# An attention with two MLPs behind it: loads wait for the landing four places ahead, and two first products move into the attention

## The chip, the core and the metric

The kernel runs on one core of a Trainium2 chip. The metric is the time of one execution in device microseconds; lower is better. The core has TensorE (PE in the profile, its weight loads PEld), VectorE (DVE), ScalarE (ACT), GpSimd (POOL) and SyncE (SP), which here only issues transfers. Every engine works through its own instructions in order, and waits on semaphores for the others.

## The reference, cut to what matters

Inputs are q, k and v of shape 2 x 8 heads x 768 x 64 in float32, a decay per head, and the weights of two MLPs of 512 x 2048 and 2048 x 512. The attention runs in blocks of 64 positions with a state that decays from block to block:

```python
for b in range(nb):
    intra = np.einsum('bhic,bhjc->bhij', qb, kb) * Dmask[None]
    intra = np.einsum('bhij,bhjd->bhid', intra, vb)
    inter = np.einsum('bhid,bhde->bhie', qb * lam_pow[None], kv_state)
    out[:, :, sl] = intra + inter
    kv_state = lam_block * kv_state + np.einsum('bhsd,bhse->bhde', kb * rev_pow, vb)
...
h = x @ w_in;  g = h * np.clip(h + 3.0, 0.0, 6.0) / 6.0;  x = g @ w_out     # first MLP
h = x @ w_in;  g = np.maximum(0.01 * h, h);               x = g @ w_out     # second MLP
```

## The kernel before

**Attention.** There are 12 chunks c of 64 positions, each with both batches and all heads. For a chunk TensorE makes three pieces of 16 matmuls each in float32: the scores s(c) into a `pair` bank (`scores`), the state t(c) into an `a` bank (`state`), and the output o(c) into an `h` bank (`attn_out`). A float32 matmul is two matmul records and two weight-load records, so a piece is 64 records. ScalarE copies q into the other halves of the pair bank before s(c) (`queries`, two copies, L314), copies t(c) beside v for the next chunk (`state_copy`, two copies, L336), copies half of an odd chunk's v (`part_v`, L289), and rounds o(c) to the high part xh of x (`att_x`, L353). VectorE masks the scores into r (`mask`, L322) and makes the low part xl. GpSimd multiplies k by the decay (`k_decay`).

**MLPs.** Tokens stand in three tiles of 512 (four chunks each), the 2048 hidden units in 16 slices f. Weights come as 64-bit floats; ScalarE reads both halves of a slice (c at L416, t at L420), VectorE composes a float32 of them in four operations, ScalarE rounds it to wh and VectorE makes the rest, wl. A product then takes three matmuls for one: wh with xh, wh with xl, wl with xh. `gemm1(s)` is the first product of one slice on one token tile, 12 matmuls of 128 x 512; then come a gate (u, Gh, Gl) and the second products into `acc` banks.

**What sets the order.** `Order` is a planner: each operation has an engine, a cost, a due time, predecessors and buffers, and the operations are written out in the order in which the planner starts them. Every engine then keeps that order, and semaphores do the rest. `due1` and `due2` are the due times of first and second products; chunk c is due at `DUE_C[c]`.

**Loads.** Loads of q and k (three of 256 KB for a chunk: q, k for the decay, k for the scores), of v (two of 256 KB for a pair of chunks) and of the first slices (two halves of 256 KB each; later slices one of 512 KB) go through SP in the order of `LOAD_ORDER`. They are numbered here from 0: 0 to 2 are q and k of chunk 0, 3 and 4 v of chunks 0 and 1, and so on. Buffers hold four chunks of q and k, three pairs of v and three raw slices. The landings are told by eight semaphores in turn, so that load n also waits for the landing of load n - 8. TensorE's records are counted (`records`), and a border is put 8 records past record 193 and every 256 records after it. From load 15 on, six loads each wait for the first matmul behind a border; the planner is told of it by `AT_BORDER`.

Of the kernel before, what the change touches and what calls it, by code (L numbers as in the profile page):

```python
# [9 lines left out]
F32 = mybir.dt.float32  # L10
# [26 lines left out]
DUE_C = [5.0 + 3.5 * c for c in range(NSC)]  # L37
T_FIRST, T_STEP, T_COLLECT, HOP = 40.0, 5.45, 2.0, 0.3
LATENCY = {"dma": 2.5, "pe": 0.15, "act": 0.15, "dve": 0.15, "pool": 0.15}
N_WARM, T_WARM = 9, 4.4  # L40
N_DENSE = {("s", 0): 5}
NQ = 4

FIRST_BORDER, BLOCK, PAST_BORDER = 193, 256, 8
FIRST_LOADS, LOADS_PER_BLOCK = 15, 6
AT_BORDER = (('o', 0), ('o', 1), ('s', 4), ('t', 4), ('o', 5), ('s', 8), ('t', 8), ('o', 9))
LOAD_ORDER = (('qk', 0), ('v', 0), ('qk', 1), ('qk', 2), ('v', 2), ('qk', 3), ('qk', 4), ('v', 4), ('qk', 5), ('qk', 6), ('v', 6), ('qk', 7), (0, 0, 0), ('qk', 8), ('v', 8), ('qk', 9), ('qk', 10), ('v', 10), (0, 0, 1), ('qk', 11))


class Order:  # L50
# [7 lines left out]
    def add(self, engines, fn, due=1e9, after=(), takes=(), frees=()):  # L58


        engines = [engines] if isinstance(engines, tuple) else engines
        self.ops.append((engines, fn, due, [a for a in after if a is not None], list(takes), list(frees)))
        return len(self.ops) - 1

    def issue(self):
# [11 lines left out]
        def start(n):  # L77
# [14 lines left out]
            for u in users[n]:  # L92
                far = e != ops[u][0][0][0]
                heapq.heappush(events, (now + us + far * LATENCY.get(e, 0.0), u, n))
            return True
# [27 lines left out]
def decay_attention_two_mlps(ctx: ExitStack, tc: tile.TileContext, qkk, vv, lam, w1, w2, out):  # L123
    nc = tc.nc
# [13 lines left out]
    od = Order({**sizes, "q": NQ, "pair": 2, **{n: 0 for n in late}, **{f"acc{e}": 0 for e in range(4)}})  # L138
    add = od.add

    def new(n, shape, dtype, name=None):
        return pool[n].tile(shape, dtype, tag=name or n, name=name or n)


    records, borders, loads = [0], [], []

    def mm(out, a, x, **flags):
        at = FIRST_BORDER + BLOCK * len(borders) + PAST_BORDER
        i = nc.tensor.matmul(out, a, x, **flags)  # L149
        if records[0] >= at:  # L150
            borders.append(i.ins)
        records[0] += 4 if a.dtype == F32 else 2

    def load(out, in_):
        i = nc.sync.dma_start(out=out, in_=in_)  # L155
        k = (len(loads) - FIRST_LOADS) // LOADS_PER_BLOCK
        loads.append(i)
        if 0 <= k < len(AT_BORDER):
            tc.add_manual_dep(i.ins, borders[min(k, len(borders) - 1)].name, mybir.DependencyInfo(
                mybir.DependencyClass.Sync, mybir.DependencyReason.DATA), reason="behind the border")  # L160

    starts = [[sum(bs[:i]) for i in range(len(bs) + 1)] for bs in BLOCKS]
    steps = [(l, b, t, f) for l in range(2) for b in range(len(BLOCKS[l])) for t in range(NTT)
# [11 lines left out]
    due_c = DUE_C  # L175
    due1 = [T_FIRST + T_STEP * s for s in range(NS)]
    due2 = [d + 1.5 * T_STEP for d in due1]

    own = [slice(0, 64), slice(64, 128)]
    other = [slice(64, 128), slice(0, 64)]  # L180
# [119 lines left out]
    def scores(c):  # L300
        def fn(_):

            ps, qk = PA["s", c], QK[c % NQ]
            for h in range(H):
                for b in range(2):
                    mm(ps[own[b], b, h, :], qk[other[b], 1, h, :], qk[other[b], 0, h, :],
                                     start=True, stop=True)
        return fn
# [29 lines left out]
    def attn_out(c):  # L338
        def fn(_):
            ps = PA["o", c] = new("h", [P, KC, 2, C], F32)  # L340
            for b in range(2):
                for h in range(H):
                    mm(ps[own[h % 2], h // 2, b, :], VS[c][:, b, h, :], R[c][:, b, h, :],
                                     start=True, stop=True)
        return fn
# [17 lines left out]
    pieces = {}  # L363
    st, copies, masks, dense_ops, att_ops = {}, {-1: []}, [], [op_warm], []
    for c in range(NSC):
# [5 lines left out]
        s = pieces["s", c] = add(pe, scores(c), d, after=[qc, op_warm])  # L371
# [10 lines left out]
        o = pieces["o", c] = add(pe, attn_out(c), d + 2.6, after=[m, ld["v", c]] + copies[c - 1], takes=["h"])  # L382
        add(("none", 0.0), nothing, after=[o, st.get(c)], frees=["vs"] * (c % 2) + ["r"])
        for n, a in (("s", s), ("t", st.get(c)), ("o", o)):
            i = N_DENSE.get((n, c), 0)
# [17 lines left out]
    def load_w(h):  # L403
        def fn(_):
            l, f, j = h
            RAW[h] = new("raw", [P, DM, 2], U32)
            raw, w = RAW[h].rearrange("p n t -> p (n t)"), (w1, w2)[l][f, j].bitcast(U32)
            for a in (slice(0, DM), slice(DM, 2 * DM)) if l + f < 2 else (slice(0, 2 * DM),):
                (load if h in LOAD_ORDER else nc.sync.dma_start)(raw[:, a], w[:, a])
        return fn  # L410

    def low_bits(h):
        def fn(_):

            CV[h] = [new("cv", [P, DM], U32, "t"), new("cl", [P, DM], U32, "c")]
            nc.scalar.activation(out=CV[h][1], in_=RAW[h][:, :, 0], func=AF.Copy, scale=2.0 ** -29)  # L416
        return fn

    def magnitude(h):
        return lambda _: nc.scalar.activation(out=CV[h][0].bitcast(F32), in_=RAW[h][:, :, 1].bitcast(F32), func=AF.Abs)  # L420

    def exponent(h):
        def fn(_):
            t = CV[h][0]

            nc.vector.tensor_scalar(out=t.bitcast(F32), in0=t.bitcast(F32), scalar1=MAG_MIN, scalar2=MAG_MAX,  # L426
                                    op0=ALU.max, op1=ALU.min)

            nc.vector.tensor_scalar(out=t, in0=t, scalar1=5, scalar2=2,
                                    op0=ALU.logical_shift_left, op1=ALU.logical_shift_right)  # L430
        return fn
# [44 lines left out]
    for l in range(2):  # L476
        for f in range(NF):
            for j in range(2):
                h = (l, f, j)
                held = paired(l, f) and j == 0  # L480
                ld_w = ld[h] = add(("dma", 1.45), load_w(h), takes=["raw"])
                a = add(("act", 0.67), low_bits(h), after=[ld_w], takes=["cv", "cl"])
                m = add(("act", 0.67), magnitude(h), after=[ld_w, a])
                x = add(("dve", 1.2 if h in LOAD_ORDER else 0.85), exponent(h), after=[m])
                c = add(("dve", 1.7 if h in LOAD_ORDER else 1.4), compose(h), after=[a, x], frees=["cl"] + ["raw"] * (not (held and f % 2)))
                composed[h] = c
                hi = add(("act", 0.62), w_high(h), after=[c], takes=[f"w{j}"])
                low[h] = w_ready[h] = add(("dve", 0.7), w_low(h), after=[hi], frees=[] if held else ["cv"])
            if paired(l, f) and f % 2:
                p, i = f // 2, None  # L490
                for n in range(4):
                    i = add(("dve", 0.43), w_sum(l, p, n), after=[composed[l, f - 1, 0], composed[l, f, 0], i])
# [3 lines left out]


    def in_order(names):
        n, behind = 0, None
        for h in names:  # L500
            op = ld["vp" if h[0] == "v" else "qk", h[1]] if len(h) == 2 else ld[h]
            k = (n - FIRST_LOADS) // LOADS_PER_BLOCK
            od.ops[op][3].extend(([pieces[AT_BORDER[k]]] if 0 <= k < len(AT_BORDER) else []) + [behind] * (behind is not None))
            n += 3 if h[0] == "qk" else 2
            behind = op
        for h in ld:
            if len(h) == 3 and h not in names:
                od.ops[ld[h]][3].append(behind)

    in_order(LOAD_ORDER)  # L510

    PH, U, G, ACC = {}, {}, {}, {}
# [311 lines left out]
    at = T_FIRST + T_STEP * n1 - 5.44  # L824
# [26 lines left out]
    for s in range(n1 - 2, NS):  # L851
        l, b, t, f = steps[s]
# [304 lines left out]
```

## Time and profile before

| | |
|---|---|
| median of 3 runs | 558.35 us (558.33 to 558.46) |
| the profiled execution's span | 559.4 us |
| TensorE busy | 547.4 us, 98% |
| VectorE busy | 431.6 us, 77% |
| ScalarE busy | 361.2 us, 65% |
| loads of q and k, issue to landing | 5.2 us, median of 36 |

The profile is one execution; its span runs from the first to the last instruction and is 1.05 us more than the median of the runs. Busy shares are means over the whole span, in which the attention takes about the first 60 us and the two MLPs the rest. The granted clock of TensorE is the full one in every slice.

### The profile page before, as it was taken

How to read it: one execution, taken by the hardware profiler on the slowest of the kernel's cores; microseconds unless marked ns; L12 is line 12 of the kernel's file. 1: busy time of each engine (PE TensorE's matmuls, PEld its weight loads, DVE VectorE, ACT ScalarE, POOL GpSimd, SP SyncE). 2: the span in 40 equal slices, each digit the busy share in tenths (PEclk: the TensorE clock that was granted, in tenths of full speed). 3: DMA queues.
4: the chain of work that ended last, by engine and by line, in shares of the span. 5: the costliest groups of instructions: out<-in, count | busy, mean ns of one | idle time of the engine just before them, and what ended most of it. 6: DMA issues, size and time to landing. Idle time of an engine off the chain costs nothing.

```text
span 559.4 us, 9243 instructions
## 1 busy us (share of the span) xinstructions
PE 547.4 (98%) x3584; PEld 462.1 (83%) x3584; DVE 431.6 (77%) x718; ACT 361.2 (65%) x634; POOL 59.7 (11%) x68
## 2 busy tenths in 40 slices
PE   8889999999999999999999999999999999999997
PEld 4788888888888888888888888888888888888885
DVE  6769999889898996878879798886467964784342
ACT  4888975668666763588668797587257744573220
POOL 6552001101101101101000000000110100110000
PEclk9999999999999999999999999999999999999999
DMA  8896325237165514334110221332332522411314
GB/s 282 268 328 222 107 87 127 39 98 204 44 164 145 138 24 109 79 110 112 51 65 0 81 108 39 113 117 72 76 76 84 143 75 45 107 43 33 76 44 108
DMA packets 24302, 59.32 MB, mean 106 GB/s; under 512 B 2882, under 2 KB 3138, under 8 KB 24258
## 3 DMA queue, kind: packets, MB, share of 16 engines
q1 hardware_dynamic: 18672, 48.77, 26.6%
q0 software_dynamic: 5184, 9.44, 10.1%
q8 instruction: 28, 0.46, 0.3%
q10 hardware_dynamic: 402, 0.52, 0.3%
q14 instruction: 16, 0.13, 0.1%
HBM read 46.14 MB, written 3.15 MB: 88 GB/s over the span
## 4 chain that ended last, share of the span: by engine, by line
PE 93%; ACT 2%; DMA 2%; issue 1%; DVE 1%; SPq 0%; ACTq 0%
PE acc L149 46%; PE h L149 28%; PE a L149 18%; DMA sums<-qkk 2%; PE pair L149 1%; ACT vs L336 1%; ACT pair L314 1%; DVE kd L251 0%; ACT xh L353 0%; DVE r L322 0%; ACT vs L289 0%; SPq L155 0%; DVE sums L1065 0%; DVE xl L351 0%; ACT t L420 0%
## 5 line engine op out<-in xcount | busy, mean ns | idle before, releaser
L568 POOL DMA_DIRECT2D sums<-st x36 | 31.8, 929 | 424.9 <-ACT st L624 408.0
L149 PE MATMUL acc<-Gh,wh 128*128 128x512 f32 x136 | 53.2, 391 | 0.0
L149 PE MATMUL acc<-Gl,wh 128*128 128x512 f32 x136 | 53.1, 390 | 0.0
L149 PE MATMUL acc<-Gh,wl 128*128 128x512 f32 x136 | 52.9, 389 | 0.0
L149 PE MATMUL acc<-wl,Gh 128*128 128x512 f32 (+1 forms) x128 | 49.6, 387 | 0.0
L149 PE MATMUL acc<-wh,Gh 128*128 128x512 f32 (+1 forms) x128 | 49.6, 387 | 0.0
L149 PE MATMUL acc<-wh,Gl 128*128 128x512 f32 (+1 forms) x128 | 49.4, 386 | 0.0
L416 ACT ACTIVATE c<-raw 128x512 uint32<-128x512 uint32 x64 | 43.0, 674 | 7.7 <-DVE t L439 5.1
L439 DVE CUSTOM_DVE_ANT_0 t<-t,c 128x1024 uint16<-128x1024 uint16 x64 | 44.3, 692 | 2.2
L626 DVE TENSOR_TENSOR sums<-acc,sums 128x512 f32<-128x512 f32 x35 | 24.1, 690 | 28.3 <-PE acc L149 28.1
L437 DVE SCALAR_TENSOR_TENSOR t<-raw,t 128x512 uint32<-128x512 uint32 x64 | 44.8, 700 | 1.0
L449 DVE TENSOR_TENSOR wl<-t,wh 128x512 fp32r<-128x512 f32 (+1 forms) x64 | 42.3, 664 | 3.0 <-ACT wh L445 2.9
L420 ACT ACTIVATE t<-raw 128x512 f32<-128x512 f32 x64 | 42.7, 666 | 0.0
L445 ACT CAST wh<-t 128x512 fp32r<-128x512 f32 (+1 forms) x64 | 37.8, 592 | 3.0 <-PE acc L149 2.3
L149 PE MATMUL h<-xh,s 128*128 128x512 f32 x112 | 38.4, 389 | 0.0
L426 DVE TENSOR_SCALAR t<-t 128x512 f32<-128x512 f32 x64 | 27.7, 433 | 12.9 <-ACT t L420 12.9
L554 DVE TENSOR_TENSOR Gl<-u,Gh 128x512 fp32r<-128x512 f32 x32 | 22.1, 689 | 17.9 <-ACT Gh L751 17.5
L757 ACT ACTIVATE u<-a 128x512 f32<-128x512 f32 x24 | 14.4, 598 | 29.1 <-PE a L149 29.1
L624 ACT COPY st<-acc 128x512 f32<-128x512 f32 x34 | 19.9, 586 | 18.8 <-PE acc L149 16.2
L149 PE MATMUL a<-xh,wl 128*128 128x256 f32 (+1 forms) x92 | 30.7, 333 | 0.0
L149 PE MATMUL a<-xl,wh 128*128 128x256 f32 (+1 forms) x92 | 30.7, 333 | 0.0
L149 PE MATMUL a<-xh,wh 128*128 128x256 f32 (+1 forms) x92 | 30.6, 333 | 0.0
(175 smaller groups left out, 1484.1 us busy)
## 6 DMA issues: line engine op xcount, KB each, us to landing
raw<-w SPq DMA_DIRECT2D x58, 512.0 KB, 3.3
sums<-qkk SPq DMA_DIRECT2D x36, 256.0 KB, 5.2
sums<-st POOLq DMA_DIRECT2D x36, 256.0 KB, 3.8
vs<-vv SPq DMA_DIRECT2D x12, 256.0 KB, 4.7
raw<-w SPq DMA_DIRECT2D x12, 256.0 KB, 4.2
out<-sums SPq DMA_DIRECT2D x19, 128.0 KB, 2.4
out<-sums ACTq DMA_DIRECT2D x3, 128.0 KB, 2.7
out<-sums SPq DMA_DIRECT2D x2, 64.0 KB, 2.3
```

The lines of the kernel that those rows point to most:

```text
L149: i = nc.tensor.matmul(out, a, x, **flags)
L416: nc.scalar.activation(out=CV[h][1], in_=RAW[h][:, :, 0], func=AF.Copy, scale=2.0 ** -29)
L420: return lambda _: nc.scalar.activation(out=CV[h][0].bitcast(F32), in_=RAW[h][:, :, 1].bitcast(F32), func=AF.Abs)
L426: nc.vector.tensor_scalar(out=t.bitcast(F32), in0=t.bitcast(F32), scalar1=MAG_MIN, scalar2=MAG_MAX, op0=ALU.max, op1=ALU.min)
L437: nc.vector.scalar_tensor_tensor(out=t, in0=RAW[h][:, :, 1], scalar=0xC0000000, in1=t, op0=ALU.bitwise_and, op1=ALU.bitwise_or)
L439: nc.vector.tensor_tensor(out=t, in0=t, in1=c, op=ALU.add)
L445: nc.scalar.copy(out=W[h][0][:, cols(*h)], in_=CV[h][0].bitcast(F32)[:, cols(*h)])
L449: return lambda e: eng[e].tensor_tensor(out=W[h][1][:, cols(*h)], in0=CV[h][0].bitcast(F32)[:, cols(*h)], in1=W[h][0].bitcast(F32)[:, cols ...
L554: nc.vector.tensor_tensor(out=gl, in0=U[s], in1=gh.bitcast(F32), op=ALU.subtract)
L568: return lambda _: nc.gpsimd.dma_start(out=SUM[t][:, e, :], in_=STAGE[t, e], accum_op=ALU.add)
L624: nc.scalar.copy(out=STAGE[t, e], in_=ps)
L626: nc.vector.tensor_tensor(out=acc, in0=ps, in1=acc, op=ALU.add)
```

## The change

The borders and their bookkeeping go. A load from number 15 on waits for the landing of the load four places ahead of it, and that holds for all weight loads too. The due times of the first two first products (slice 0 on token tiles 0 and 1) are set to 20 and 34, where they were 40 and 45.45, and the load of slice 0's input weights (0, 0, 0) moves from behind qk 7 to behind v 4: its halves are now loads 21 and 22; v of chunks 8 and 9 are loads 37 and 38 before and after. Line numbers from here on are lower by 7 to 9 after the change; matmuls, which all stood at line 149, now carry the lines of the functions that make them.

```diff
--- before.py
+++ after.py
@@ -37,14 +37,13 @@
 DUE_C = [5.0 + 3.5 * c for c in range(NSC)]
 T_FIRST, T_STEP, T_COLLECT, HOP = 40.0, 5.45, 2.0, 0.3
 LATENCY = {"dma": 2.5, "pe": 0.15, "act": 0.15, "dve": 0.15, "pool": 0.15}
+T_AHEAD = [20.0, 34.0]
 N_WARM, T_WARM = 9, 4.4
 N_DENSE = {("s", 0): 5}
 NQ = 4
 
-FIRST_BORDER, BLOCK, PAST_BORDER = 193, 256, 8
-FIRST_LOADS, LOADS_PER_BLOCK = 15, 6
-AT_BORDER = (('o', 0), ('o', 1), ('s', 4), ('t', 4), ('o', 5), ('s', 8), ('t', 8), ('o', 9))
-LOAD_ORDER = (('qk', 0), ('v', 0), ('qk', 1), ('qk', 2), ('v', 2), ('qk', 3), ('qk', 4), ('v', 4), ('qk', 5), ('qk', 6), ('v', 6), ('qk', 7), (0, 0, 0), ('qk', 8), ('v', 8), ('qk', 9), ('qk', 10), ('v', 10), (0, 0, 1), ('qk', 11))
+FIRST_LOADS, IN_FLIGHT = 15, 4
+LOAD_ORDER = (('qk', 0), ('v', 0), ('qk', 1), ('qk', 2), ('v', 2), ('qk', 3), ('qk', 4), ('v', 4), (0, 0, 0), ('qk', 5), ('qk', 6), ('v', 6), ('qk', 7), ('qk', 8), ('v', 8), ('qk', 9), ('qk', 10), ('v', 10), (0, 0, 1), ('qk', 11))
 
 
 class Order:
@@ -142,22 +141,15 @@
         return pool[n].tile(shape, dtype, tag=name or n, name=name or n)
 
 
-    records, borders, loads = [0], [], []
-
-    def mm(out, a, x, **flags):
-        at = FIRST_BORDER + BLOCK * len(borders) + PAST_BORDER
-        i = nc.tensor.matmul(out, a, x, **flags)
-        if records[0] >= at:
-            borders.append(i.ins)
-        records[0] += 4 if a.dtype == F32 else 2
+    loads = []
+    mm = nc.tensor.matmul
 
     def load(out, in_):
         i = nc.sync.dma_start(out=out, in_=in_)
-        k = (len(loads) - FIRST_LOADS) // LOADS_PER_BLOCK
-        loads.append(i)
-        if 0 <= k < len(AT_BORDER):
-            tc.add_manual_dep(i.ins, borders[min(k, len(borders) - 1)].name, mybir.DependencyInfo(
-                mybir.DependencyClass.Sync, mybir.DependencyReason.DATA), reason="behind the border")
+        loads.append(i.ins)
+        if len(loads) > FIRST_LOADS:
+            tc.add_manual_dep(i.ins, loads[-1 - IN_FLIGHT].name, mybir.DependencyInfo(
+                mybir.DependencyClass.Sync, mybir.DependencyReason.DATA), reason="so many in flight")
 
     starts = [[sum(bs[:i]) for i in range(len(bs) + 1)] for bs in BLOCKS]
     steps = [(l, b, t, f) for l in range(2) for b in range(len(BLOCKS[l])) for t in range(NTT)
@@ -175,6 +167,7 @@
     due_c = DUE_C
     due1 = [T_FIRST + T_STEP * s for s in range(NS)]
     due2 = [d + 1.5 * T_STEP for d in due1]
+    due1[:len(T_AHEAD)] = T_AHEAD
 
     own = [slice(0, 64), slice(64, 128)]
     other = [slice(64, 128), slice(0, 64)]
@@ -406,7 +399,7 @@
             RAW[h] = new("raw", [P, DM, 2], U32)
             raw, w = RAW[h].rearrange("p n t -> p (n t)"), (w1, w2)[l][f, j].bitcast(U32)
             for a in (slice(0, DM), slice(DM, 2 * DM)) if l + f < 2 else (slice(0, 2 * DM),):
-                (load if h in LOAD_ORDER else nc.sync.dma_start)(raw[:, a], w[:, a])
+                load(raw[:, a], w[:, a])
         return fn
 
     def low_bits(h):
@@ -496,12 +489,10 @@
 
 
     def in_order(names):
-        n, behind = 0, None
+        behind = None
         for h in names:
             op = ld["vp" if h[0] == "v" else "qk", h[1]] if len(h) == 2 else ld[h]
-            k = (n - FIRST_LOADS) // LOADS_PER_BLOCK
-            od.ops[op][3].extend(([pieces[AT_BORDER[k]]] if 0 <= k < len(AT_BORDER) else []) + [behind] * (behind is not None))
-            n += 3 if h[0] == "qk" else 2
+            od.ops[op][3].extend([behind] * (behind is not None))
             behind = op
         for h in ld:
             if len(h) == 3 and h not in names:
```

On TensorE the first product moves ahead. Before, these rows lead to it; `a` is a state piece, `h<-r` an output piece and `pair` a scores piece, and the last two rows are the first matmuls of the product on token tile 0:

```order
L149 MATMUL a<-vs,kd_105 64x64 x16
L149 MATMUL h<-r,vs 64x64 x16
L149 MATMUL pair<-sums 64x64 x16
L149 MATMUL a<-vs,kd_104 64x64 x16
L149 MATMUL h<-r,vs 64x64 x16
L149 MATMUL pair<-sums 64x64 x16
L149 MATMUL a<-vs,kd_105 64x64 x16
L149 MATMUL h<-xh_107,wh 128x512
L149 MATMUL h<-xl_108,wh 128x512
```

After, it stands behind s6; the first row here is o3, and the rows of one product are cut after the third:

```order
L336 MATMUL h<-r,vs 64x64 x16
L324 MATMUL a<-vs,kd_105 64x64 x16
L299 MATMUL pair<-sums 64x64 x16
L324 MATMUL a<-vs,kd_104 64x64 x16
L336 MATMUL h<-r,vs 64x64 x16
L299 MATMUL pair<-sums 64x64 x16
L516 MATMUL h<-xh_107,wh 128x512
L516 MATMUL h<-xl_108,wh 128x512
L516 MATMUL h<-xh_107,wl 128x512
```

Thirteen pieces that stood ahead of the product now stand behind it, and o3 stands ahead of t3. The product on token tile 1 moves likewise, from behind s11 to behind s9.

On ScalarE the rows between the pair copies of s4 (first row) and of s5 were these before:

```order
L314 COPY pair<-sums 64x512 x2
L336 COPY vs<-a 64x512 x2
L289 COPY vs<-vs 64x512
L353 CAST xh_107<-h 128x4x128
L314 COPY pair<-sums 64x512 x2
L336 COPY vs<-a 64x512 x2
```

After, both readings of slice 0 (c, t) and the cast for chunk 3 stand between them as well:

```order
L307 COPY pair<-sums 64x512 x2
L329 COPY vs<-a 64x512 x2
L409 ACTIVATE c<-raw 128x512
L413 ACTIVATE t<-raw 128x512
L346 CAST xh_107<-h 128x4x128
L282 COPY vs<-vs 64x512
L346 CAST xh_107<-h 128x4x128
L307 COPY pair<-sums 64x512 x2
L329 COPY vs<-a 64x512 x2
```

So the pair copies of s5 have moved behind two readings, a cast and a copy of v; the last row is the copies of t3.

On SP, the rows from the v of chunks 4 and 5 on, before (`x6` are two chunks of q and k, `raw` is a slice):

```order
L155 DMA vs<-vv 128x512 x2
L155 DMA sums<-qkk 128x512 x6
L155 DMA vs<-vv 128x512 x2
L155 DMA sums<-qkk 128x512 x3
L155 DMA raw<-w 128x512 x2
L155 DMA sums<-qkk 128x512 x3
L155 DMA vs<-vv 128x512 x2
```

And after:

```order
L148 DMA vs<-vv 128x512 x2
L148 DMA raw<-w 128x512 x2
L148 DMA sums<-qkk 128x512 x6
L148 DMA vs<-vv 128x512 x2
L148 DMA sums<-qkk 128x512 x6
L148 DMA vs<-vv 128x512 x2
L148 DMA sums<-qkk 128x512 x6
```

The two halves of slice 0 have moved ahead of nine loads of q and k and two of v.

## Rows read from the trace of the kernel before

**Rows 1.** Windows: stretch, length, busy PE, PEld, DVE, ACT, POOL; clock, DMA.

```profile
10.00:60.00 50.00, 44.46 (x1092) 39.28 (x1092) 39.54 (x47) 41.96 (x74) 22.00 (x20) 1.00 0.76 255
60.00:80.00 20.00, 20.00 (x116) 16.67 (x115) 19.57 (x33) 18.11 (x33) 0.00 (x0) 1.00 0.39 132
```

**Rows 2.** Waits of PE from 0 to 60 us: total, times, longest.

```profile
PE pair L149 <- issue: 1.9, 2, 1.7
PE a L149 <- issue: 1.4, 2, 1.3
PE h L149 <- issue: 0.9, 1, 0.9
PE a L149 <- DVE kd L251: 0.8, 1, 0.8
PE pair L149 <- ACT pair L314: 0.3, 1, 0.3
PE a L149 <- ACT vs L336: 0.3, 1, 0.3
```

**Rows 3.** Timeline of PE: start, us, work, idle time before it.

```profile
21.80 0.44 PE L149 MATMUL pair<-sums 64*64 64x64 f32 x7
23.94 0.27 PE L149 MATMUL pair<-sums 64*64 64x64 f32 x2 [1.70 <-issue]
...
48.93 0.34 PE L149 MATMUL a<-vs,kd 128*64 128x64 f32 x4 [1.26 <-issue]
```

**Rows 4.** The page: its first line, and the DMA queue of code.

```profile
span 559.4 us, 9243 instructions
...
q8 instruction: 28, 0.46, 0.3%
```

**Rows 5.** DMA views of 16.5-21.4, 21.4-22.4 and 50.2-51.2 us, in turn (q8: code).

```profile
DMA packets 818, 1.50 MB, mean 306 GB/s; under 512 B 87, under 2 KB 87, under 8 KB 818
...
q8 instruction: 1, 0.02, 5.5%
...
DMA packets 10, 0.04 MB, mean 37 GB/s; under 512 B 4, under 2 KB 4, under 8 KB 9
q8 instruction: 1, 0.02, 6.0%
```

**Rows 6.** Loads issued at 0.75, 14.20 and 52 us: us to landing; SP's timeline.

```profile
sums<-qkk SPq DMA_DIRECT2D x1, 256.0 KB, 2.7
...
sums<-qkk SPq DMA_DIRECT2D x1, 256.0 KB, 4.7
14.20 1.54 SPq L155 DMA_DIRECT2D sums<-qkk  x1
...
raw<-w SPq DMA_DIRECT2D x2, 256.0 KB, 3.3
```

**Rows 7.** The chain: start, length, work (one piece; one product).

```profile
19.71 1.08 PE pair L149 x32
...
84.99 2.72 PE h L149 x12
```

**Rows 8.** Timeline of ACT.

```profile
20.84 1.18 ACT L336 COPY vs<-a 64x512 f32<-64x512 f32 x2
...
34.12 0.67 ACT L416 ACTIVATE c<-raw 128x512 uint32<-128x512 uint32 x1 [1.65 <-DMA raw<-w]
```

**Rows 9.** Groups of ACT, 10 to 50 us: count, busy us, mean ns, idle before.

```profile
L314 ACT COPY pair<-sums 64x512 f32<-64x512 f32 x19 | 11.1, 584 | 0.9 <-DVE r L322 0.4
L353 ACT CAST xh<-h 128x512 fp32r<-128x512 f32 x9 | 5.2, 581 | 0.0
L289 ACT COPY vs<-vs 64x512 f32<-64x512 f32 x5 | 3.1, 616 | 0.1
L416 ACT ACTIVATE c<-raw 128x512 uint32<-128x512 uint32 x2 | 1.4, 686 | 1.6 <-DMA raw<-w 1.6
L420 ACT ACTIVATE t<-raw 128x512 f32<-128x512 f32 x2 | 1.4, 684 | 0.0
```

## The prediction

> **What bounds the kernel now.** I read the windows first. From 60 to 80 us TensorE is busy 20.00 of 20 us, and VectorE 19.57 beside it; from 10 to 60 us TensorE is busy only 44.46 of 50 and ScalarE 41.96 [rows 1]. So the matrix stages are bound by TensorE, and all that a reordering of loads can win lies in the attention, the first 60 us. Next, the list of TensorE's waits there [rows 2]: 1.9 + 1.4 + 0.9 = 4.2 us are put down to "issue", a wait for nothing that the profile shows; 0.8 us to the decay rows that VectorE makes; 0.3 + 0.3 us to ScalarE's copies. The rest (2.3 us) lies before the first data and no edit touches it.
>
> What are the 4.2 us? The timeline shows two of them: TensorE stops in the middle of a piece at 22.24 (21.80 + 0.44) and goes on at 23.94, and stops again until 48.93 [rows 3]. A piece is 64 instruction records, and the stops lie 256 records or a multiple apart. The page counts 28 transfers of kind "instruction" on queue q8, 0.46 MB in all, so 16 KB each [rows 4]; TensorE's 3584 matmuls and 3584 weight loads are 7168 = 28 x 256 records. One such transfer is a block of TensorE's code. The DMA views place them: one lies from 21.4 to 22.4 us, with 1.50 MB of other traffic in the 4.9 us ahead of it, and TensorE goes on 1.5 us after that; the one asked for at 48.93 lies from 50.2 to 51.2 [rows 5]. I read it so: a block's transfer is asked for when TensorE enters the block before it, and waits behind loads already queued. The block that ends at 22.24 was entered four pieces of 1.08 us [rows 7] and the 0.8 us of the decay rows earlier, so at about 17.1, with the queue full of loads: the transfer came 4.3 us later. The one after 48.93, when the loads run dry (0.04 MB of all traffic in that microsecond), came 1.3 us later. The transfer itself takes 5.5% of 16 engines over 1.0 us, 0.9 us [rows 5].
>
> **The change part by part.** *The wait of each load.* Today a load waits for a product behind a code border, and otherwise for the landing eight places ahead (the semaphores' own limit); now for the landing four ahead. A load into an empty queue lands after 2.7 us, one in the crowd after 4.7 [rows 6]. With four in flight a code transfer should wait between the 1.3 us seen when loads run dry and half of the 4.3 seen with a full queue, so 1.3 to 2.2 us. Adding 0.9 for the transfer and 1.5 to go on gives 3.7 to 4.6 us, against 4 pieces x 1.08 us [rows 7] = 4.3 us in which TensorE uses up a block. The stops nearly vanish: at best all 4.2 us go, at worst 0.3 us stay at each of the four blocks that hold pieces alone, 1.2 us. I leave 0.3 us, since the middle, 4.2, is just below 4.3.
>
> What is queued behind a waiting load is every later load. Three raw buffers already keep weight loads to three slices at once, so behind the attention the new wait is met before it is reached: 0. Output stores stand behind the last load and lose nothing.
>
> *The moved products.* Two products of the first slice (12 matmuls each, 2.72 us as a block in the chain [rows 7]) go from behind the attention pieces to places inside. TensorE's work is the same, so this costs and gains nothing by itself; it slows the use of code there. But the work that feeds them moves too, above all on ScalarE, which runs in order. Between the copies of t2 and the pair copies of s5 it now has both readings of the raw weights. In the trace the copies of t2 end at 20.84 + 1.18 = 22.02 [rows 8]. Then stand c and t (0.69 + 0.68), two xh casts (2 x 0.58), one copy of v (0.62) and the pair copies (2 x 0.58) [rows 9]: 4.3 us, 26.3. TensorE has s4 from 21.80, then o3 and t3, and without the code stop is free at 21.80 + 3 x 1.08 = 25.0. So s5 waits at least 1.3 us.
>
> Also c waits for the second half of the weights, load 22 of the new order. Load 18 lands at 14.2 + 4.7 = 18.9 [rows 6], and I leave that, as its predecessors don't move. Load 22 is issued then, takes 2.7, and one code transfer (0.9) is served in between: 22.5. That is 0.5 us after ScalarE is ready: s5 waits 1.8. That such a wait does hit what stands behind it, the trace shows: ScalarE sat idle 1.65 us before c at 34.12, for the raw weights [rows 8].
>
> The next place is t6. From s5 (26.8) TensorE has s5, t4, o4, s6, the product, t5, o5, s7: 7 x 1.08 + 2.72 = 10.3, so 37.1. ScalarE has behind the pair copies of s5: two pairs of copies of t, two of pair, wh, xh, v: 4 x 1.18 + 3 x 0.6 = 6.5, so 33.3; then the copy of v8, which needs load 38; then pair copies, a gate and the copies of t5, 0.6 + 1.2 + 0.7 + 1.2 = 3.7. Load 38 lands four rounds after load 22, 22.5 + 4 x 2.7 + 0.9 = 34.2. So the copies end at 37.9 and t6 waits 0.8 us. Bounds: if v8 is there in time 37.0, no wait; if a lone load takes 3.3 us, as one did [rows 6], load 22 lands at 23.1 and load 38 at 37.2: s5 waits 2.4 us and t6 3.2.
>
> VectorE's part of the slice, and its wl that the product's third matmul needs, now run beside the decay products of GpSimd; by the same sum wl comes about when TensorE reaches it. I take 0.2 us, from 0 to 0.9. The product holds one of two h banks until its gate; o5 has the other: 0.
>
> The sum: -4.2 - 0.6 (ScalarE's old waits, whose copies come out anew) + 0.3 + 1.8 + 0.8 + 0.2 = -1.7 us. The profiled execution spans 559.4 us [rows 4], 1.05 above the median of the runs, 558.35. So 557.7 for the span, 556.7 for the median. One thing pulls back: between 60 and 80 us VectorE is idle 0.43 us in 20. If its work there doesn't start earlier by as much as TensorE does, TensorE waits for it. VectorE has 10 us idle between 10 and 60 [rows 1] and takes its first slice earlier now, so I expect most of the lead to hold and take 0.3 us: 557.0.
>
> One rule of the Trainium skill speaks against the first step: "DMA: Bandwidth & Descriptors", section on queues, rings and completion order, has each engine round-robin between its queue rows at packet granularity. By it a code transfer wouldn't wait behind the loads at all, and fewer loads in flight would give back none of the 4.2 us. The 4.3 us with a full queue against 1.3 us with a short one speak for waiting behind loads [rows 5], so the sum goes by those.
>
> **The rivals.** (a) *The stops stay*: code transfers are late for a cause other than the queue's depth. Then 4.2 us stay, ScalarE's new waits lie partly under them (the stop of 1.70 us falls just before s5), and about 2.8 - 1.7 - 0.6 = +0.5 to +2 us come on top: 559.6. For it: the transfer at 21.4 came after the loads then queued should have been through, and its delay is the largest of all. By the round-robin rule of the Trainium skill this is the case that comes out. (b) *Slower by late loads*: at four in flight every round costs a full latency, and v8 comes late. It decides when load 38 lands after about 36.7 instead of 34.2, for 1.4 us of lead and 1.1 us for a verdict go then. Rounds of 3.3 us, and code transfers that cost 1.3 each, put load 22 at 23.5 and load 38 at 38.0: s5 waits 2.8 us, t6 3.6, and the sum is -4.8 + 0.3 + 6.4 + 0.2 = +2.1: 560.4. For it: a load of the same size after the attention took 3.3 us [rows 6]; against it: 2.7 at the start. (c) *Given back behind the attention*: VectorE, 98% busy from 60 to 80 us, doesn't start earlier; then only its 0.43 us of idle time can be won there, 557.9. (d) *ScalarE's waits don't come*, as loads run ahead of my walk: -4.8 + 0.3 + 1.3 = -3.2 us, 555.2.
>
> **How the numbers follow.** The forecast (0.8 to 2.5 us gained) has 0.40, (d) 0.10, (c) 0.25, (b) 0.17, (a) 0.08. The time is the forecast's, 557.0; its own range is 555.9 to 557.6. From below (d) to most of (b) the range is 554.8 to 560.0. 0.2% is 1.1 us, about what a measurement of this kernel can tell from no change: faster means under 557.2, slower over 559.5. Faster: (d) and most of the forecast, 0.10 + 0.36. Same: (c) and the rest of the forecast, 0.25 + 0.04. Slower: (a) and (b), 0.08 + 0.17.
>
> **What would show it.** In the profile after, TensorE's "issue" waits in the first 60 us should add up to under 1 us, and a code transfer should follow its border by 1.3 to 2.3 us. The wait of TensorE's pair piece for ScalarE's pair copies should be 1.3 to 2.4 us near 25, and that of an a piece for the vs copies up to 1 us near 37. Issue to landing of qkk should fall from a median near 5 us to near 3. From 60 to 540 us TensorE should have no wait. Issue waits of 3 us or more mean (a); ScalarE waiting for loads for more than 3 us means (b); waits for Gl or wl behind 60 us mean (c). The prediction is wrong altogether if the load stream of the attention ends later than today.

## The result, and the profile after

The change made the kernel slower: 563.70 us (562.93 to 565.08, four runs) against 558.34 (558.28 to 558.46), a ratio of 1.0099 (95% interval 1.0084 to 1.0114). Forecast were 557.0 us and a range of 554.8 to 560.0. The profiled execution after took 563.51 us, with a span of 561.7; first the page's rows, TensorE's busy time, the granted clock in 40 slices, and the loads:

```profile
span 561.7 us, 9233 instructions
...
PE 548.9 (98%) x3584; PEld 464.5 (83%) x3584; DVE 431.3 (77%) x718; ACT 361.1 (64%) x634; POOL 60.7 (11%) x68
...
PEclk9988999999999999999999999999999999999999
...
sums<-qkk SPq DMA_DIRECT2D x36, 256.0 KB, 3.9
```

The clock row was 9 throughout before. Next the windows of after that answer to [rows 1], the stretch of the loads from 18 to 50 us, and four of 2 us each (columns as there; the third from the right is the granted clock, the last GB/s):

```profile
10.00:60.00 50.00, 42.91 (x1031) 39.13 (x1029) 35.51 (x42) 39.59 (x69) 22.53 (x20) 0.93 0.78 253
60.00:80.00 20.00, 19.74 (x142) 16.24 (x137) 19.52 (x34) 18.27 (x34) 0.00 (x0) 1.00 0.32 107
18.00:50.00 32.00, 25.37 (x575) 23.14 (x570) 21.47 (x25) 22.43 (x39) 12.85 (x12) 0.89 0.85 269
...
28.00:30.00 2.00, 2.00 (x40) 1.88 (x38) 1.73 (x4) 1.94 (x4) 0.00 (x0) 0.50 0.94 313
30.00:32.00 2.00, 2.00 (x48) 1.93 (x46) 1.83 (x2) 1.36 (x4) 1.40 (x2) 0.66 0.96 300
...
42.00:44.00 2.00, 2.00 (x43) 2.00 (x41) 1.88 (x3) 0.96 (x3) 0.23 (x1) 0.50 0.97 284
44.00:46.00 2.00, 2.00 (x53) 1.93 (x51) 1.97 (x2) 1.50 (x4) 1.93 (x2) 0.75 0.76 249
```

From 10 to 60 us TensorE does less in the same time than before, and twice its clock is at 0.50, the lower of its two levels (1.2 GHz). Before, the same stretch of loads moved more:

```profile
18.00:50.00 32.00, 26.72 (x738) 24.50 (x739) 24.12 (x27) 26.51 (x48) 15.17 (x14) 1.00 0.91 303
```

What TensorE waits for, from 0 to 60 us, the list that answers to [rows 2]:

```profile
PE pair L299 <- ACT pair L307: 2.4, 1, 2.4
PE a L324 <- issue: 2.2, 1, 2.2
PE h L336 <- issue: 1.5, 2, 1.0
...
PE pair L299 <- issue: 0.8, 1, 0.8
PE a L324 <- ACT vs L329: 0.3, 1, 0.3
```

The first row is s5. The second is put down to "issue", but is no stop for code: it is t6, and TensorE's timeline beside ScalarE's shows what it waits for (start, length, work, idle time before):

```profile
27.14 1.34 PE L299 MATMUL pair<-sums 64*64 64x64 f32 x32 [2.44 <-ACT pair L307]
28.40 1.97 PE L324 MATMUL a<-vs,kd 128*64 128x64 f32 x32
...
41.11 0.30 PE L324 MATMUL a<-vs,kd 128*64 128x64 f32 x2 [2.16 <-issue]
41.66 1.86 PE L324 MATMUL a<-vs,kd 128*64 128x64 f32 x29 [0.26 <-ACT vs L329]
```

```profile
22.86 0.69 ACT L409 ACTIVATE c<-raw 128x512 uint32<-128x512 uint32 x1 [2.88 <-DMA raw<-w]
...
25.89 1.20 ACT L307 COPY pair<-sums 64x512 f32<-64x512 f32 x2
...
37.85 0.61 ACT L282 COPY vs<-vs 64x512 f32<-64x512 f32 x1 [3.54 <-DMA vs<-vv]
...
40.43 1.18 ACT L329 COPY vs<-a 64x512 f32<-64x512 f32 x2
```

ScalarE stands 2.88 us for the second half of the weights (load 22, landed 22.78) and 3.54 us for the v of chunk 9 (load 38, landed 37.83). Its pair copies for s5 end at 27.09, its copies for t6 at 41.01 and 41.61; TensorE starts 0.05 to 0.1 us after each. So both waits of TensorE begin at a load, and each time ScalarE stands at an instruction that the waiting piece doesn't use: at the weights ahead of s5, and ahead of t6 at a copy of v that only the pieces of chunk 9 use. Part of the wait of s5 would stay without that: its own k (load 25) landed at 26.00, 1.3 of the 2.4 us after t3.

Real stops for code are left at two blocks, 0.46 us (in the third row) and 0.77 us, 1.2 us in all. The other 1.0 us of the third row is o3, and this wait begins at a load too. o3 waits for the mask of s3, the first of the two in the last row below, and VectorE is late with it because it stood 2.56 us for the v of chunk 4 (load 19, landed 20.81):

```profile
22.61 1.15 PE L336 MATMUL h<-r,vs 128*64 128x64 f32 x32 [1.00 <-issue]
...
20.83 0.42 DVE L282 COPY vs<-vs 64x512 f32<-64x512 f32 x1 [2.56 <-DMA vs<-vv]
21.29 2.36 DVE L315 TENSOR_TENSOR r<-pair,decay 128x1024 f32<-128x1024 f32 x2
```

The stop of 0.77 us lies ahead of o3, in s4, and only shortens this wait.

### The profile page after: what moved, and what is told of

It reads as the page before. It is cut to its first block, busy times and chain, and to the rows that moved or that the text cites. A ratio compares the mean times of both kernels' runs of the same rounds, so it can differ in the third digit from the quotient of the medians.

```text
span 561.7 us, 9233 instructions
## 1 busy us (share of the span) xinstructions
PE 548.9 (98%) x3584; PEld 464.5 (83%) x3584; DVE 431.3 (77%) x718; ACT 361.1 (64%) x634; POOL 60.7 (11%) x68
## 4 chain that ended last, share of the span: by engine, by line
PE 90%; DMA 4%; ACT 2%; POOL 1%; DVE 1%; issue 0%; SPq 0%; DVEq 0%
PE acc L604 45%; PE h L692 20%; PE a L692 14%; PE h L516 5%; DMA sums<-qkk 2%; PE a L516 2%; DMA vs<-vv 1%; POOL kd L289 1%; PE a L604 1%; ACT vs L329 1%; DMA raw<-w 1%; PE h L336 1%; PE a L324 1%; ACT pair L307 0%; PE pair L299 0%
## 5 line engine op out<-in xcount | busy, mean ns | idle before, releaser
L604 PE MATMUL acc<-wl,Gh 128*128 128x512 f32 x124 | 48.5, 391 | 0.0
L604 PE MATMUL acc<-wh,Gh 128*128 128x512 f32 x124 | 48.4, 391 | 0.0
L604 PE MATMUL acc<-wh,Gl 128*128 128x512 f32 x124 | 48.2, 389 | 0.0
L432 DVE CUSTOM_DVE_ANT_0 t<-t,c 128x1024 uint16<-128x1024 uint16 x64 | 45.8, 715 | 2.2
L604 PEld LDWEIGHTS acc<-Gh,wl 128*128 128x128 f32 x136 | 25.5, 188 | 5.4
L604 PEld LDWEIGHTS acc<-Gh,wh 128*128 128x128 f32 x136 | 25.6, 188 | 5.3 <-DVE r L315 0.4
L604 PEld LDWEIGHTS acc<-Gl,wh 128*128 128x128 f32 x136 | 25.6, 188 | 4.8
```

Of the source, the lines that this page charges most:

```text
L432: nc.vector.tensor_tensor(out=t, in0=t, in1=c, op=ALU.add)
L604: mm(ACC[e], a, x, start=(first and n == 0 and not seeded(s, e)), stop=(last and n == 2), skip_group_check=seeded(s, e))
```

## The experiments

All are timed beside the kernel before on the same chip. There its runs lie between 556.45 and 563.37 us with medians of 558.0 to 558.9, wider than in the runs shown first; each ratio is against the runs of before that stand beside it. A profile shows one execution, and not the median one: it took 567.42 us for the first kernel of the table, 560.17 for the second, 565.05 for the third, 559.92 for five in flight and 566.15 for the order of before without waits.

| kernel | us, median | ratio to before (95%) |
|---|---|---|
| four in flight, order of before | 566.31 | 1.014 (1.012 to 1.016) |
| products moved, borders kept | 558.85 | 1.0017 (1.0000 to 1.0033) |
| the change, waits filled with products of zeros | 563.92 | 1.0102 (1.0084 to 1.0119) |
| the change, eight in flight | 557.55 | 0.9985 (0.9969 to 1.0001) |
| the change, six in flight | 558.78 | 1.0009 (0.9993 to 1.0024) |
| the change, five in flight | 561.04 | 1.0041 (1.0025 to 1.0057) |
| order of before, no waits | 561.84 | 1.0064 (1.0040 to 1.0087) |
| products moved, borders, one wait filled | 558.95 | 1.0008 (0.9986 to 1.0031) |
| four in flight up to load 38 | 565.21 | 1.0110 (1.0082 to 1.0138) |
| four in flight from load 39 | 558.06 | 0.9992 (0.9970 to 1.0014) |
| eight in flight, products later | 559.25 | 1.0015 (0.9996 to 1.0034) |
| four in flight, v of chunks 8 and 9 earlier | 566.01 | 1.0095 (1.0058 to 1.0132) |
| four in flight, larger loads | 560.03 | 1.0019 (0.9995 to 1.0043) |

### The kernel before, a second profile

No edit.

> The kernel before once more, unchanged, for a second profile of it. In its first profile load 2 lands at 6.76 us and s0 starts at 6.90; in the profile after load 2 lands at 5.10 and s0 starts at 5.65, though no edit touches the first 15 loads, and by s4 the two stand 2.37 us apart (21.80 against 19.43). Theory: the first profile of before caught a late start that its timed runs don't have. Then this one has s0 near 5.65, s4 near 19.4 and a span of 556 to 557.5 at a time of 558.3. Rival: the late start belongs to this kernel, s0 is near 6.90 again and the span 559.

It took 558.79 us with a span of 557.0. The page's first rows and the waits:

```profile
span 557.0 us, 9243 instructions
...
PE 547.1 (98%) x3584; PEld 462.1 (83%) x3584; DVE 430.9 (77%) x718; ACT 361.3 (65%) x634; POOL 59.8 (11%) x68
```

```profile
PE a L149 <- issue: 1.0, 2, 0.8
...
PE h L149 <- issue: 0.7, 1, 0.7
...
PE pair L149 <- issue: 0.2, 1, 0.2
```

Half right. The late start is here too (s0 at 6.73), so it doesn't explain the base. What differs is the stops for code: 1.9 us in place of the 4.2 of [rows 2], and that is nearly the whole difference of the spans, 2.4 us. And the time of an execution is its span plus 1.8 us: 558.79 against 557.0 here, 563.51 against 561.7 after. The execution that the prediction was made from, with its span of 559.4, must by this have taken about 561.2 us (an estimate). It was one of the long ones.

### Each half of the change alone

Four in flight with the order of before:

```diff
-T_AHEAD = [20.0, 34.0]
+T_AHEAD = []
-LOAD_ORDER = (..., ('v', 4), (0, 0, 0), ('qk', 5), ('qk', 6), ('v', 6), ('qk', 7), ('qk', 8), ...)
+LOAD_ORDER = (..., ('v', 4), ('qk', 5), ('qk', 6), ('v', 6), ('qk', 7), (0, 0, 0), ('qk', 8), ...)
```

> The wait for the landing four places ahead alone: no borders, due times and load order of before. Theory A (the moved products lose the time, by two waits of TensorE for ScalarE and a granted clock of 0.50 for 3.3 us behind each): no wait for ScalarE over 1 us, clock 1.00 all through, and of the 4.2 us of stops near 1.2 stay: 558.3 - 3.0 = 555.3, from 554.5 to 558. Theory B (four loads in flight are too few, data come late): the last load of the attention lands at 51 us or later, as in the change, and the time is 560 or more.

And the products with their load moved, in the kernel before, borders kept:

```diff
+T_AHEAD = [20.0, 34.0]
...
+    due1[:len(T_AHEAD)] = T_AHEAD
```

> The two products and the load of slice 0 moved alone; the loads wait at the borders as before. TensorE's order is that of the change. Theory A: TensorE waits near 2 us for ScalarE's pair copies ahead of s5, the granted clock falls to 0.50 for some 3 us, and the time is 561 to 565. Theory B: with the loads as early as before the waits are short, the clock stays at 1.00, and the time is 557 to 559.5.

By the times theory A falls and B stands; the clock of the moved products wasn't at 1.00 in their profiled execution (0.85 from 20 to 30 us). Four loads in flight in place of the borders cost 8.3 us in the old order (566.31 - 558.04), more than the whole change, and some 3.5 us of it go with the borders (see the order of before without any wait, below); the moved products alone cost nothing that can be told (558.85). The last load of the attention landed at 52.30 with four in flight and the old order, 51.06 in the change, 48.43 and 48.09 in the two profiles of before; but also at 50.17 with the products moved alone, so this landing doesn't tell the time by itself. With four in flight ScalarE stands for loads in the old order too:

```profile
28.30 0.61 ACT L282 COPY vs<-vs 64x512 f32<-64x512 f32 x1 [2.10 <-DMA vs<-vv]
...
34.98 0.66 ACT L409 ACTIVATE c<-raw 128x512 uint32<-128x512 uint32 x1 [3.15 <-DMA raw<-w]
```

TensorE then stood 3.01 us before t6. So four in flight make TensorE wait in either order, though not at the same places, and with the products moved the loss is even smaller (563.7 against 566.3). What the order does set is when a load is needed. In the first profile of before load 38 landed at 37.34, hardly earlier than in the change, and nobody waited for it, as ScalarE came to its copy only at 40.06:

```profile
40.06 0.62 ACT L289 COPY vs<-vs 64x512 f32<-64x512 f32 x1
```

In the change ScalarE is ready for that copy 5.8 us earlier, at 34.3 (37.85 - 3.54).

### Is it the clock?

```diff
+N_FILL = {("s", 5): 10, ("t", 6): 9}
...
+            fill(N_FILL.get(("s", c), 0))
...
+            fill(N_FILL.get(("t", c), 0))
```

> The change with products of zeros set into TensorE's two waits: ten ahead of s5, nine ahead of t6, 0.22 us each at full clock, into a bank that nobody reads. They can't make the data come sooner. Theory A: TensorE doesn't idle, the clock stays at 1.00, and what the half clock took, 2 x 1.65 us, comes back: 563.7 - 3.3 = 560.4, from 559.5 to 561.3. Rival: what follows the waits is held by loads anyway, so that a faster clock only makes the next wait longer: 562.7 or more, with waits of 1.5 us or more that weren't there.

The rival came out, 563.92 us. Behind s5 the clock held (1.00 from 28 to 40 us, TensorE busy all 12 us), but the work done earlier only met the next late load:

```profile
39.01 2.12 PE L204 MATMUL a<-zeros 128*128 128x512 bf16 x9
43.85 1.97 PE L333 MATMUL a<-vs,kd 128*64 128x64 f32 x32 [2.72 <-issue]
```

```profile
40.01 0.61 ACT L289 COPY vs<-vs 64x512 f32<-64x512 f32 x1 [5.04 <-DMA vs<-vv]
```

ScalarE now stood 5.04 us for load 38, which landed at 39.99. This profile alone settles nothing: elsewhere the clock still fell (0.83 as the mean of 20 to 30 us, behind a stop of 1.99 us, and of 40 to 50), and from 10 to 60 us it is 0.93 as in the change. The other executions say more, by the mean granted clock that each shows. It was 0.993 in the profiled one (565.05 us, the longest of five), and 0.999 in one of 563.88 us, in which by that figure less than 1 us of work was lost. So with next to no half clock the time is still that of the change, and the old order with four in flight took 565.97 and 566.64 us at 0.999; of the change's own four runs the one at 0.997 took 563.90 us and the one at 0.992 took 562.93. The same filling where loads are not the chain, in the kernel with the products moved and the borders kept, seven ahead of s5:

> The products moved alone, borders kept, with seven products of zeros ahead of s5, where TensorE waited 1.40 us for the pair copies and its granted clock then fell (0.85 in 20 to 30 us, 0.98 in 30 to 40: 1.7 us of work). Clock theory: the clock stays at 1.00 and, as the loads are not the chain here, the work comes back: 558.85 - 1.6 = 557.3, from 556.8 to 558. Rival: what follows waits for something else anyway, 558.4 to 559.5.

There the clock did stay at 1.00 all through, where it had been 0.85 from 20 to 30 us, and the time was 558.95 against 558.85: nothing came back. But this test says little: of the twelve runs with the products moved eleven had a granted clock of 0.999 or more without any filling, and the profiled one (0.997, 560.17 us) was the exception. In the filled profile there are stops for code of 1.2 and 1.6 us and a wait of 1.4 us for xl. The half clock is seen, but it isn't what the change loses.

### How many loads in flight

```diff
-FIRST_LOADS, IN_FLIGHT = 15, 4
+FIRST_LOADS, IN_FLIGHT = 15, 8
```

> The change with 8 in place of 4 loads in flight, which is the semaphores' own limit: the wait has no effect, and no borders either. Theory L (the stream of loads is the chain of the change; with four in flight it moves 269 GB/s from 18 to 50 us against 303 and 307 in the two profiles of before): load 22 lands before 21.8 us in place of 22.78, load 38 before 35.5 in place of 37.83, and the time is 557 to 559.5, as with the products moved alone and the borders kept. Rival S (without any wait the code blocks stand behind a full queue): issue waits of 4 us or more, 560 to 563.

> The change with six loads in flight. Theory L: nearly the full stream, load 38 near 35.5 to 36.5, 558 to 560.5, between eight and four. Rival S: if eight brings back the stops, six is faster than eight by 1 us or more.

> The change with five in flight, between four (563.7) and six (558.8). If the loss comes of lateness that decides once load 38 lands later than about 36.7 us, five (38 lands near 35.5) is near six, 558.5 to 560. If the loss grows evenly with every load less in flight, 561 to 562.

Eight: 557.55, six: 558.78, five: 561.04, four: 563.70. By the time theory L holds at eight and six; load 38 landed at 31.30 and 33.70. At five the median was already 2.3 us over before (558.72 beside it), in the range named for an even loss; load 38 landed at 35.37 in the profile, which is of one of the shorter executions (559.92). That speaks against a sharp point at 36.7 and doesn't exclude it. By the medians each load less costs more than the one before; the intervals are too wide to show it. That eight differs from before isn't shown, as its interval reaches 1.0001. In its waits s5 stands 1.0 us, and stops are 1.4 and 0.5 us:

```profile
PE pair L299 <- issue: 1.4, 1, 1.4
...
PE pair L299 <- ACT pair L307: 1.0, 1, 1.0
...
PE h L336 <- issue: 0.5, 1, 0.5
```

The order of before without any wait, neither borders nor a number in flight:

> The order of before without borders and with 8 in flight, so without any wait of a load but for buffers and semaphores. With four in flight this order took 566.3. Theory L: the 8 us come back, 557.5 to 560; what is left over 558.0 is what the borders are worth. Rival S: 561 or more, with issue waits of 4 us or more.

561.84, with two stops that add up to 5.7 us:

```profile
PE pair L299 <- issue: 5.7, 2, 3.2
```

So rival S is right for the old order and wrong for the new one. The old order without borders is 3.5 us slower than with them (558.38 beside it): that is what the borders were worth there. The 5.7 us are those of the longest of six executions (566.15 us), so most likely more than the median holds. With the full queue the new order is 4.3 us faster (561.84 - 557.55), with stops of 1.9 us in its profile. That the products among the pieces give the code time to come, as 12 matmuls fill 2.7 us with 24 records [rows 7], would explain it and isn't shown: the load of slice 0 and ScalarE's order moved as well.

### Which loads

Four in flight for loads 15 to 38 only, and for those from 39 on only:

```diff
-        if len(loads) > FIRST_LOADS:
+        if FIRST_LOADS < len(loads) <= 39:
...
-        if len(loads) > FIRST_LOADS:
+        if len(loads) > 39:
```

> The change, but four in flight for loads 15 to 38 alone; the later ones go eight in flight. Theory L1 (the time is lost in the first part, where load 22 feeds the reading ahead of s5 and load 38 the v ahead of t6): load 38 lands at 37 or later and the time stays at 562 to 564. L2 (it is the end of the stream, load 51 at 51.06 us, that holds the end of the attention): most comes back, 557.5 to 560.

> The other half: eight in flight up to load 38, four from load 39 on, the weight loads behind the attention among them. L1: load 38 lands before 32.5 as with eight everywhere (31.30), and the time is 557 to 559. L2: 561 or more.

L1: 565.21 with four early (1.2 us above its range), 558.06 with four late. The whole loss comes of loads 15 to 38, and none that can be told of the later ones, the weight loads behind the attention among them. With four early, ScalarE stands 4.40 us for load 38, TensorE 4.3 before t6:

```profile
39.42 0.61 ACT L282 COPY vs<-vs 64x512 f32<-64x512 f32 x1 [4.40 <-DMA vs<-vv]
```

### One late load, or the stream?

```diff
-LOAD_ORDER = (..., ('v', 6), ('qk', 7), ('qk', 8), ('v', 8), ('qk', 9), ...)
+LOAD_ORDER = (..., ('v', 6), ('v', 8), ('qk', 7), ('qk', 8), ('qk', 9), ...)
```

(The planner's predecessor of that load is changed to fit.)

> The change with the two loads of v of chunks 8 and 9 put ahead of the q and k of chunks 7 and 8 (six places earlier), four in flight as before; TensorE's and ScalarE's orders are those of the change. If the wait ahead of t6 (2.2 and 0.3 us, and the half clock behind it) comes of ScalarE standing 3.54 us before the copy of v8 for load 38, then v8 is there, t6 starts near 39.5 in place of 41.66, and some 2.2 us come back before the v of chunk 10 is late next (it lands at 47.40): 561.5, from 560.5 to 562.3. If the stream as a whole holds the end, the loads put back cost what v8 wins: 563 to 564.5.

The step came out and the time didn't: t6 starts at 39.45 without a wait, and the next load of v is late in its place, so that the second product waits 2.3 us for xh and 1.1 more for xl:

```profile
39.45 1.42 PE L324 MATMUL a<-vs,kd 128*64 128x64 f32 x31
```

```profile
47.20 0.61 ACT L282 COPY vs<-vs 64x512 f32<-64x512 f32 x1 [3.35 <-DMA vs<-vv]
```

566.01 us: no better than the change, and above what was named for either case. So no single load holds the time; the wait moves on to the next late one. The other remedy, a later place for ScalarE's and VectorE's copies of v in their own orders, wasn't tried.

### Bytes, or the count of loads?

```diff
-            for i in (0, 2, 1):
+            for i in (slice(0, 3, 2), slice(1, 2)):
...
-            for i in range(2):
-                load(vp[:, i, 0], vv[c + i])
+            load(vp[:, :, 0], vv[c:c + 2].rearrange("i p h d -> p i h d"))
```

(and the first slices as one load each, `FIRST_LOADS` 9.)

> The change with larger loads: q with the decay's k in one of 512 KB and the other k in one of 256 KB, v of two chunks in one of 512 KB, slice 0 and 1 in loads of 512 KB; four in flight still, from the same place on. If four loads of 256 KB are too few bytes on the way for the time that a load needs, twice the bytes bring the stream back (over 290 GB/s from 18 to 50 us in place of 269) and the time to 557.5 to 560, as with seven or eight small ones. If it is the count, with longer loads taking longer in proportion: under 275 GB/s, 562 or more.

560.03 us, and the stream is back:

```profile
18.00:50.00 32.00, 26.39 (x626) 23.37 (x624) 23.80 (x30) 27.27 (x47) 13.77 (x13) 1.00 0.86 297
```

297 GB/s with four in flight, as the loads are larger; the time is just above what was named for this case, and it isn't told apart from before. The window alone doesn't rank kernels: with eight small loads in flight, which are done sooner, it shows 281, and with four early 296 at 565.21 us. The landings agree, though: the v of chunk 11 landed at 41.59 here, at 47.40 in the change and at 40.67 with eight. It is the bytes on the way that were too few, and not the count of loads.

### Later products

```diff
-T_AHEAD = [20.0, 34.0]
+T_AHEAD = [30.0, 42.0]
```

(with eight in flight.)

> Eight in flight with due times of 30 and 42 in place of 20 and 34, so that the first reading of the weights stands behind the pair copies of s5's neighbours and not both readings ahead of them. If the 1.0 us that TensorE still waits for the pair copies of s5 with eight in flight is a real loss: no such wait, 556 to 557.2. Rival: with fewer products among the pieces code is used up faster and a stop of 2 us or more comes in the second half, as the order of before had without waits (3.2 us at 43 us): 558.5 to 561.

559.25 us, the rival by the time: the pair copies are waited for 0.6 us in place of 1.0, but stops add up to 4.0 in the profile, an execution of 560.93 us (1.06, 1.70 and 1.20), though none of 2 us in the second half. No kernel here is shown to beat the one before.

## Why the prediction was wrong

**The base.** The sum set its -4.2 us against a span of 559.4, "1.05 above the median of the runs". A run's time is its span plus 1.8 us, so that execution lay about 2.8 us above the median (559.4 + 1.8 - 558.35), and its stops were most of that. In the second profile the stops are 1.9 us; the change leaves 1.2. The term of -4.2 + 0.3 was worth -0.7 against that profile. Three times of before stood beside the profile, and none of them was the time of the profiled execution; taking them for it was the error.

**The round of four.** This is the step of the mechanism that failed: "Load 38 lands four rounds after load 22, 22.5 + 4 x 2.7 + 0.9 = 34.2". Load 22 landed at 22.78, but load 38 at 37.83: 3.8 us a round. Loads 26, 30, 34 and 38 each went out within 0.1 us of the landing four places ahead, so that nothing but the limit held them, and took 4.1, 3.1, 3.6 and 4.1 us. Either of the two errors turns the sign alone: with 1.9 + 0.6 us for 4.2 + 0.6 the sum is +0.6, and with the measured 2.4 and 2.4 us for the waits of 1.8 and 0.8 it is +0.5. 2.7 us was the time of a load into an empty queue [rows 6], and taken for that of one among four. The median of the q and k loads was 3.9 us, and four loads of 0.262 MB in 3.9 us are 269 GB/s, just what the window from 18 to 50 us moved, against 303 before (where eight in 5.2 us would be 403, so that the number in flight wasn't the limit). The Trainium skill ("DMA: Bandwidth & Descriptors", section on the anatomy of one DMA, there for the path through GpSimd) gives about 2.0 us plus the bytes at 436 GB/s for one DMA, an estimate of 2.6 us here; that fits the lone load, and makes the same error as the prediction if it is used for four at a time. Why four take 3.9 us and not 2.7 is shown only so far: in the trace of after they land in bursts (20.81, 21.48, 22.14, 22.78) with a hole of some 1.4 us behind (load 27, which waits for the next of them, went out at 24.25), and twice the bytes in each load bring the rate back. What sets the holes stays open.

**The waits.** s5 waited 2.4 us (forecast 1.8, bounds 1.3 to 2.4), t6 2.2 and 0.3 (0.8, bounds 0 to 3.2). The places, the releasers and the chain through ScalarE were as forecast (its "copy of v8" is that of chunk 9). The 1.0 us of o3, behind VectorE's copy of a late v, had no term. Rival (b), late loads, is what came: load 38 landed after 36.7 us, ScalarE stood 6.4 us for loads where 3 were its sign, and the stream ended later than before (51.06 against 48.43), the sign of being wrong altogether. It had a chance of 0.17 because the empty queue's 2.7 us was held against it. It priced the two waits at 2.8 and 3.6 us, more than they were, and still gave too little: its sum took 4.8 us off for stops and old waits. With the second profile's 1.9 + 0.6 us in their place its +2.1 becomes +4.4, beside the 4.7 by which the span grew from that profile. That it comes so near is in part luck, as the next paragraph shows.

**The sum, against the second profile.** The span grew by 4.7 us (561.7 - 557.0). TensorE's idle time grew by 2.9 (12.8 against 9.9, span less busy), its busy time by 1.8 (548.9 - 547.1). In the idle time 5.8 us of waits for late loads (2.4, 2.4 and 1.0) and 0.3 us behind 60 us are new; gone are 0.7 us of stops, ScalarE's old 0.6, and two waits of the second profile that the sum had left standing, 1.1 us for VectorE's decay rows and 1.0 us for the first data, whose loads no edit touched. That makes 2.7 of the 2.9. The busy time grew most likely by the half clock, which in the four windows above lost 3.2 us of work (2 us times 0.50, 0.34, 0.50 and 0.25); profiles without it differ by up to 2.1 us among themselves (545.3 to 547.4), so the two figures can't be matched more closely. No term of the sum had the clock. It can't simply be added to the waits, though: a filled execution at 0.999 took as long as the change.

**What else held.** That nothing is lost behind the attention (four from load 39 on: 558.06). That code comes sooner with four loads in flight: in the old order the stops are 0.8 us with four and 5.7 with eight, and from 16 to 46 us a code transfer begins at most 1.6 us after TensorE passes a block border (counted by its records) with four, and up to 5.3 us with eight. In the new order the profiles with four show 1.2 to 2.3 us of stops, those with five, six and eight 3.0, 3.2 and 1.9; one execution each doesn't order them, and the 1.2 left in the change are more than the 0.3 of the sum and the 1 us announced. That the products cost and gain nothing by themselves held with the borders (558.85); without waits of loads the new order gains 4.3 us. The late code of the old order without any wait speaks for code standing behind loads, and against the round-robin rule of the Trainium skill that was weighed there, as far as two executions can.

## What to carry to other kernels

Before a gain is taken from one profile, set that execution's own time beside the runs: a stall that varies from run to run looks largest in the profile of a long one. A limit on loads in flight is a limit on bandwidth, bytes in flight over the time of one load, and that time has to be read from loads in a stream and not from a lone one. When one late load is moved forward and the time stays, the wait has moved on to the next one; here more bytes on the way helped. And an engine that keeps its order hands a late load on to pieces that don't need it: ask of every instruction that moves ahead what stands behind it.

## What the runs showed of the hardware

- The granted clock of TensorE fell to 0.50 behind stretches in which it idled much: from 20 to 28 us it was busy 3.9 of 8 us, then the clock stood at 0.50 from 28 to 31 us and came back while TensorE was busy without a break. A stop of 1.70 us in the first profile of before left it at 1.00 [rows 3]; one of 1.70 us with the later products was followed by 0.50 from 24 to 26 us. So the length of the last stop doesn't decide it. The Trainium skill ("TensorE: Matmul & The Clock Gate", Part 1) gives the clock gate two states, 1.2 and 2.4 GHz, and the rows show these two levels.
- The same kernel stops 4.2 us for its code in one execution and 1.9 in another. Whether that makes the spread of its runs (556.45 to 563.37 us) isn't shown.
- In every execution of after and of the experiments the time was 1.8 us more than the span (1.73 to 1.86).
